# A new unit order, shared row slots and single softmax passes in a grouped-query attention forward and backward kernel

## The chip, the cores and the metric

The kernel runs on one core of a Trainium2 chip. The metric is device time in microseconds (us). Repeated runs of one kernel agree within about 0.3%. "Before" is the kernel before the change, "after" the kernel with it. The granted TensorE clock was 0.98 of full speed.

A few names for the reader. The core has a matrix engine (PE, with PEld for its weight loads), a vector engine (DVE), a scalar engine (ACT), a small general one (POOL), and SP, which here only issues DMA transfers, in program order, to one queue. A queue hands each transfer to 16 DMA engines. "Landing" is the moment when one of those 16 reports its share of a transfer as done.

## The reference, cut to what matters

```python
B, Hq, Hkv, Sq, Sk, D = 32, 32, 4, 4, 2048, 128          # all bf16

def _fwd_reference(q, k, v):
    k = jnp.repeat(k, Hq // Hkv, axis=1)
    v = jnp.repeat(v, Hq // Hkv, axis=1)
    scores = jnp.einsum("bhqd,bhkd->bhqk", q, k) * D ** -0.5
    p = _softmax(scores, axis=-1)
    return jnp.einsum("bhqk,bhkd->bhqd", p, v)

def reference(q, k, v, grad_out):
    out, vjp = jax.vjp(_fwd_reference, q, k, v)
    return (out, *vjp(grad_out))                          # out, dq, dk, dv
```

K and V are 2 MiB each per batch (four heads of 2048 x 128), and so are dK and dV. The rest is small. So 136.31 MB must be read and 136.31 MB written, and a batch moves a little over 8 MiB.

## The kernel before

The work of a batch is cut into units: LK and LV load K and V, each in two rows of 1 MiB (128 partitions x 8 KB); KT and VT transpose them on PE; S makes the scores, MX their maximum, EX the exponential, L the sum and its reciprocal; O and DQ are the small outputs; DV and DK make dV and dK in PSUM; units that end in "e" copy PSUM to SBUF on ACT or DVE; DVs and DKs store. The order of all units, over all batches and engines, is fixed by tables of times.

```python
CAP = dict(q=4, k=8, v=4, qdt=4, kt=8, vt=7, e=2, ..., out=6)     # buffers of each kind
PERIOD = 21.3
PLACE = dict(LK=[-16.977, -14.467], LV=[3.599, 0.95], ..., DVs=[39.32, 39.758], DKs=[48.837, 48.854], ...)
SHIFT = { 0: ..., 1: ..., 2: ..., -4: ..., -3: ..., -2: ..., -1: ... }   # corrections, first and last batches
... # SWAP, BANK: engine and PSUM bank of each unit

def plan(n_batches):
    ...
            u.at = b * PERIOD + PLACE[name][i] + (SHIFT[special][name][i] if special in SHIFT else 0.0)
    ...
    return sorted(order, key=lambda u: u.at), bank_of

        if name in ("LK", "LV"):
            ...
            for w in (slice(0, C * D), slice(C * D, row)) if b == 0 else [slice(0, row)]:
                nc.sync.dma_start(out=x[:, w], in_=src[g][b][:, w])
        ...
        elif name == "MX":                       # twice a batch, two PSUM banks (1024 columns) each
            nc.vector.tensor_scalar(out=spent, in0=t["S", i][:], scalar1=-scale,
                                    scalar2=t["m"][:] if i else None, op0=ALU.mult, op1=ALU.min, accum_out=m[:])
        elif name == "EX":                       # twice a batch
            nc.scalar.activation(out=t["e"][:, 2 * QW * i:2 * QW * i + 2 * QW], in_=t["S", i][:], func=ACT.Exp,
                                 bias=t["m"][:], scale=scale, accum_out=t["l2"][:, i:i + 1])
        elif name == "L":
            nc.vector.reduce_sum(out=lsum[:], in_=t["l2"][:], axis=AX.X)
            ...
        elif name in ("O", "DQ"):                # many small matmuls
            for c in range(4 * i, 4 * i + 4):
                for h in range(NH):
                    nc.tensor.matmul(t[name][r, 0:D], lhsT=left[:, j % 4, r, odd], rhs=right[:, j, :, odd], ...)
        ...
        elif name in ("DVh", "DKh"):             # the last batch only: stores in halves
            nc.sync.dma_start(out=heads_of(out)[:, :, c], in_=heads_of(x)[:, :, c])
        elif name in ("DVs", "DKs"):
            nc.sync.dma_start(out=(dv_r if name == "DVs" else dk_r)[g][b][:, 0:row],
                              in_=staged(b, name[:2])[g][:, 0:row])
```

All loads and stores go through `nc.sync`, one queue in program order. A store that waits for its data therefore also holds up every load behind it. K has 8 rows of buffer, V 4, and dV and dK together 6. Both kernels give PE 8768 matmuls, each preceded by a weight load: 17,536 instructions.

## Time and profile before

| | before |
|---|---|
| time, median of 4 runs | 680.97 us (680.24 to 681.62) |
| profiled span | 678.7 us |
| busy PE, ACT, DVE | 596.6, 593.0, 556.1 us |
| bytes by the data queue | 272.65 MB, 97.6% of 16 engines' span |

The page of the profiled run, before. Part 1 is busy time with its share of the span, part 2 the span in 40 equal slices of 17 us (GB/s is what the DMA engines moved in each), part 3 the queues (q1 carries the data, q8 is the queue that fetches PE's instructions), part 5 the groups of instructions:

```profile
span 678.7 us, 20970 instructions
PE 596.6 (88%) x8768; PEld 409.5 (60%) x8768; DVE 556.1 (82%) x777; ACT 593.0 (87%) x921; POOL 39.5 (6%) x102
...
GB/s 348 398 388 388 424 424 421 426 422 425 423 424 425 424 425 423 424 424 424 426 423 426 423 425 423 418 410 421 424 424 417 421 376 396 352 360 317 400 268 316
...
q1 hardware_dynamic: 39472, 272.65, 97.6%
q8 instruction: 68, 1.11, 0.6%
...
L409 ACT ACTIVATE e_sb<-psum,m 128x1024 bf16<-128x1024 f32 x64 | 71.1, 1121 | 6.5 <-DVE kt_sb L400 6.2
L400 DVE TENSOR_SCALAR_CACHE_REDUCE kt_sb<-psum,m 128x1024 bf16<-128x1024 f32 x32 | 41.1, 1283 | 9.4 <-PE psum L393 5.0
```

No compute engine is busy more than 88% of the span, and the data queue is at 97.6%: this kernel is limited by its transfers. The strip says where it is worse than that. Slices 4 to 31 move 421 to 426 GB/s with few exceptions; the first four move 348 to 398, and the last eight 268 to 400. The Trainium skill ("DMA: Bandwidth & Descriptors", section Bandwidth) gives 425 GB/s for a 16 MB transfer of a single core, so the middle looks as if nothing could be had there.

The last 84 us more closely, in the DMA view of that stretch (each of the 40 slices is 2.1 us):

```profile
DMA  9999999999409999999999998798104999989960
GB/s 377 428 267 413 294 384 415 423 430 418 188 23 374 381 302 409 365 300 413 431 430 417 417 433 376 298 423 341 52 20 195 433 393 369 378 326 389 380 220 2
```

And what SP's queue waited for from 530 us to the end (in total, how often, the longest):

```profile
SPq L499 <- DVE dk_sb L487: 31.6, 4, 13.9
SPq L499 <- ACT dk_sb L487: 22.5, 5, 8.6
SPq L499 <- ACT dv_sb L487: 22.5, 6, 7.8
```

L499 is the store of dV and dK. In the tail the stores wait up to 13.9 us for their data, loads stand behind them, and near 618 and 655 us the DMA engines move almost nothing (23, then 52 and 20 GB/s).

### The profile page before, as it was taken

Reading aid. Unit: us, or ns where it says so; the run is one execution under the profiler, and the core shown is the slowest. Engines: PE = TensorE matmul, PEld = TensorE weight load, DVE = VectorE, ACT = ScalarE, POOL = GpSimd, SP = SyncE. Lnnn points to the kernel's source line nnn. Section 1 sums busy time; section 2 is a strip of 40 time slices with the busy share of each in tenths; the row PEclk is TensorE's granted clock in tenths of the full one; section 3 lists DMA queues with packets and bytes.
Section 4 is the critical chain, followed back from the end, with each engine's and each line's share of the span. In section 5 each row is a group of like instructions: output and inputs, shape, how many; then the busy total and the mean of one; then the engine's idle time right before and its main releaser. Section 6 shows DMA issues by size and latency. Waiting matters only on the chain. (4 is left out here: it accounts for less than half of the span.)

```text
span 678.7 us, 20970 instructions
## 1 busy us (share of the span) xinstructions
PE 596.6 (88%) x8768; PEld 409.5 (60%) x8768; DVE 556.1 (82%) x777; ACT 593.0 (87%) x921; POOL 39.5 (6%) x102
## 2 busy tenths in 40 slices
PE   4989999999999898988899888899888887987995
PEld 3656666666666665656566656666556654655653
DVE  2799899888888888788888888788888884886896
ACT  2799999999999888988889988899988895986994
POOL 0000000000000000000000000000000000000000
PEclk9899999999999999999999999899999996997999
DMA  9999999999999999999999999999999999998968
GB/s 348 398 388 388 424 424 421 426 422 425 423 424 425 424 425 423 424 424 424 426 423 426 423 425 423 418 410 421 424 424 417 421 376 396 352 360 317 400 268 316
DMA packets 39568, 273.98 MB, mean 404 GB/s; under 512 B 4657, under 2 KB 4657, under 8 KB 7729
## 3 DMA queue, kind: packets, MB, share of 16 engines
q1 hardware_dynamic: 39472, 272.65, 97.6%
q8 instruction: 68, 1.11, 0.6%
q14 instruction: 28, 0.22, 0.1%
HBM read 136.31 MB, written 136.31 MB: 402 GB/s over the span
## 5 line engine op out<-in xcount | busy, mean ns | idle before, releaser
L382 PE MATMUL psum<-ident,v_sb 128*128 128x128 f32 x1024 | 153.5, 283 | 24.6 <-DMA v_sb<-in_v_dram 22.4
L487 ACT CAST dk_sb<-psum 128x1024 bf16<-128x1024 f32 x159 | 159.6, 1035 | 16.9 <-PE psum L482 15.2
L487 ACT CAST dv_sb<-psum 128x1024 bf16<-128x1024 f32 x155 | 152.3, 1035 | 2.7 <-PE psum L482 2.5
L382 PEld LDWEIGHTS psum<-ident,v_sb 128*128 128x128 f32 x1024 | 114.2, 143 | 66.9 <-issue 32.8
L382 PE MATMUL psum<-ident,k_sb 128*128 128x128 f32 x1024 | 145.0, 281 | 9.1 <-ACT dk_sb L487 8.0
L382 PEld LDWEIGHTS psum<-ident,k_sb 128*128 128x128 f32 x1024 | 114.2, 142 | 34.8 <-ACT dk_sb L487 19.9
L487 DVE CAST dv_sb<-psum 128x1024 bf16<-128x1024 f32 x101 | 122.6, 1218 | 2.8 <-PE psum L482 1.8
L487 DVE CAST dk_sb<-psum 128x1024 bf16<-128x1024 f32 x97 | 115.7, 1219 | 2.5 <-PE psum L482 2.2
L341 ACT COPY kt_sb<-psum 128x512 f32<-128x512 f32 x190 | 107.8, 601 | 6.5 <-PE psum L382 6.0
L472 DVE SCALAR_TENSOR_TENSOR ds_sb<-psum,delta,e_sb 128x1024 bf16<-128x1024 f32 x64 | 82.1, 1282 | 26.5 <-ACT vt_sb L341 21.3
L341 ACT COPY vt_sb<-psum 128x512 f32<-128x512 f32 x131 | 76.2, 604 | 26.5 <-PE psum L382 24.9
L344 DVE COPY vt_sb<-psum 128x1024 bf16<-128x1024 bf16 x125 | 82.9, 681 | 1.7 <-PE psum L382 1.1
L409 ACT ACTIVATE e_sb<-psum,m 128x1024 bf16<-128x1024 f32 x64 | 71.1, 1121 | 6.5 <-DVE kt_sb L400 6.2
L482 PE MATMUL psum<-e_sb,dop_sb 32*128 32x512 bf16 x512 | 62.5, 385 | 8.9 <-ACT dv_sb L487 8.3
L482 PE MATMUL psum<-ds_sb,qp_sb 32*128 32x512 bf16 x512 | 63.8, 387 | 2.9 <-DVE ds_sb L472 1.5
L344 DVE COPY kt_sb<-psum 128x1024 bf16<-128x1024 bf16 x66 | 44.9, 686 | 16.4 <-PE psum L382 16.1
L417 POOL TENSOR_SCALAR dop_sb<-k_sb,rinv 128x128 bf16<-128x128 bf16 x32 | 20.0, 626 | 613.5 <-PE psum L432 437.6
L400 DVE TENSOR_SCALAR_CACHE_REDUCE kt_sb<-psum,m 128x1024 bf16<-128x1024 f32 x32 | 41.1, 1283 | 9.4 <-PE psum L393 5.0
L432 PE MATMUL psum<-ident,ds_sb 128*128 128x128 f32 x256 | 41.2, 286 | 7.8 <-ACT e_sb L409 7.6
L482 PEld LDWEIGHTS <-dop_sb 32*128 32x128 bf16 x512 | 19.1, 91 | 43.1 <-issue 39.6
L446 PE MATMUL psum<-k_sb,dt_sb 128*32 128x128 bf16 x2048 | 43.5, 221 | 1.8 <-DVE dk_sb L487 0.7
L446 PEld LDWEIGHTS <-dt_sb 128*32 128x32 bf16 x2048 | 37.7, 95 | 11.3 <-issue 8.2
(42 smaller groups left out, 525.3 us busy)
## 6 DMA issues: line engine op xcount, KB each, us to landing
v_sb<-in_v_dram SPq DMA_DIRECT2D x62, 1024.0 KB, 20.4
k_sb<-in_k_dram SPq DMA_DIRECT2D x31, 1088.0 KB, 20.4
out_dram<-dk_sb SPq DMA_DIRECT2D x32, 1024.0 KB, 19.4
out_dram<-dv_sb SPq DMA_DIRECT2D x31, 1056.0 KB, 18.5
k_sb<-in_k_dram SPq DMA_DIRECT2D x31, 1024.0 KB, 20.4
out_dram<-dv_sb SPq DMA_DIRECT2D x31, 1024.0 KB, 20.4
out_dram<-dk_sb SPq DMA_DIRECT2D x30, 1056.0 KB, 18.1
v_sb<-in_v_dram SPq DMA_DIRECT2D x4, 512.0 KB, 8.5
```

The source lines that it names most:

```text
L341: nc.scalar.copy(out=out.rearrange("p c d -> p (c d)").bitcast(FP32), in_=in_.rearrange("p c d -> p (c d)").bitcast(FP32))
L344: nc.vector.tensor_copy(out=out, in_=in_)
L382: nc.tensor.transpose(out=ps[:, j, :], in_=src[:, 4 * i + j, :], identity=ident32[:])
L400: nc.vector.tensor_scalar(out=spent, in0=t["S", i][:], scalar1=-scale, scalar2=t["m"][:] if i else None, op0=ALU.mult, op1=ALU.min, accum_ ...
L409: nc.scalar.activation(out=t["e"][:, 2 * QW * i:2 * QW * i + 2 * QW], in_=t["S", i][:], func=ACT.Exp, bias=t["m"][:], scale=scale, accum_o ...
L417: nc.gpsimd.tensor_scalar(out=t["dop"][:], in0=t["go"], scalar1=t["rinv"][:], scalar2=None, op0=ALU.mult)
L432: nc.tensor.transpose(out=ps[:, j, :], in_=src[:, 4 * i + j, :], identity=ident32[:])
L446: nc.tensor.matmul(t[name][r, 0:D], lhsT=left[:, j % 4, r, odd], rhs=right[:, j, :, odd], start=(c == 0), stop=(c == C - 1), tile_position ...
L472: nc.vector.scalar_tensor_tensor(out=t["ds"][:, w], in0=t["DP", i][:], scalar=t["dl"][:], in1=t["e"][:, w], op0=ALU.subtract, op1=ALU.mult)
L482: nc.tensor.matmul(accs[h // 2][:, QW * (h % 2):QW * (h % 2) + QW], lhsT=t[rhs][r, :], rhs=t[lhs][r, QW * i:QW * i + QW], start=True, stop ...
L487: copy(out=heads_of(staged(b, name[:2])[g])[:, :, QW * i:QW * i + QW], in_=t[name[:2], i][g][:].rearrange("p (h c) -> p h c", h=2))
```

## The change

The change replaces the tables by one string with the order of all 3232 units. Loads and stores now alternate (per batch: SV0, LK1, SK0, LV1, LK0, SK1, SV1, LV0). K, V, dV and dK share 20 row slots in place of separate pools. MX and EX each take one pass over four PSUM banks, so the extra sum goes. q rides on one K row and grad_out on the other, out on a dV row and dq on a dK row, so the last batch's halves and the extra dq transfer go: 260 transfers in place of 267. The number of bytes and of matmuls is the same.

```diff
-CAP = dict(q=4, k=8, v=4, ..., out=6)
-PERIOD = 21.3
-PLACE = dict(...)
-SHIFT = {...}
-SWAP = {...}
-BANK = [...]
+SLOTS, E_TILES, DS_TILES = 20, 2, 2
+TILES = dict(KT=8, VT=7, ET=2, DT=2)
+PLAN = (
+    "a000a110b120a030b040a150e400f4A0e011f0A0e702f7A0e513f5A0b160a070e224f2A0e135f1D0c000d0D0e316f3A0g720h7A0e637f6A0"
...
+slots = [const_pool.tile([P, LONG], BF16, name=f"row{i}") for i in range(SLOTS)]
...
         elif name == "MX":
-            nc.vector.tensor_scalar(out=spent, in0=t["S", i][:], scalar1=-scale,
-                                    scalar2=t["m"][:] if i else None, op0=ALU.mult, op1=ALU.min,
-                                    accum_out=m[:])
+            nc.vector.tensor_scalar(out=t["e"][:], in0=t["S"], scalar1=-scale, scalar2=None, op0=ALU.mult,
+                                    op1=ALU.min, accum_out=t["m"][:])
         elif name == "EX":
-            nc.scalar.activation(out=t["e"][:, 2 * QW * i:2 * QW * i + 2 * QW], in_=t["S", i][:], func=ACT.Exp,
-                                 bias=t["m"][:], scale=scale, accum_out=t["l2"][:, i:i + 1])
-        elif name == "L":
-            nc.vector.reduce_sum(out=lsum[:], in_=t["l2"][:], axis=AX.X)
+            nc.scalar.activation(out=t["e"][:], in_=t["S"], func=ACT.Exp, bias=t["m"][:], scale=scale,
+                                 accum_out=t["l"][:])
...
-        elif name in ("DVh", "DKh"):
-            ...
-        elif name in ("DVs", "DKs"):
-            ...
+        elif name in ("SV", "SK"):
+            n = LONG if i else ROW
+            nc.sync.dma_start(out=(dv_r if name == "SV" else dk_r)[i][b], in_=t["D" + name[1], "out", i][:, 0:n])
```

## The prediction

> **What bounds the kernel now.** The DMA queue. The page shows the queue at 97.6% of 16 engines' span, 272.65 MB in a 678.7 us span, and the 40-slice strip shows 421 to 426 GB/s in most slices from 5 to 31. The Trainium skill ("DMA: Bandwidth & Descriptors", section Bandwidth) gives 425 GB/s for large single-core transfers; this trace agrees (424), so the body is at the queue's rate. In the list of DMA issues, the middle batches (200 to 540 us) repeat every 20.52 us, each transfer of 1 MiB landing about 2.45 us (loads) or 2.6 us (stores) after the one before, seven others always outstanding (latency 20.4 us = 8 transfers). Compute is faster: from 110 to 205 us, when it set the pace, a batch took 19.3 us. Busy per batch: PE 18.6, ACT 18.5, DVE 17.4 us.
>
> **Where time is lost now.** 32 x 20.52 = 657 us is the estimated pure queue time; the span is 678.7. The loss is at both ends: 398, 388, 388 GB/s in slices 1 to 4, and 376, 396, 352, 360, 317, 400, 268, 316 in the last eight. In the tail the SP queue waits for stores' data (single waits of 8 to 14 us) while loads stand behind it in order; the backlog falls to nothing near 572, 582, 594, 619, 648 and 658 us, and PE twice waits 4 to 6 us for k_sb.
>
> **What the change does.**
> - Bytes: unchanged (272.6 MB). The middle cannot get faster than the queue.
> - Loads and stores alternate mostly one by one, and 20 rows are shared by K, V, dV and dK in place of 8+4+6 in separate pools. Loads stay roughly 2.5 batches ahead. This should keep the queue filled in the head and most of the tail: the main gain.
> - One EX over 2048 columns: two cost 2 x (1121+209) ns; one about 2200 (estimate from the column slope of the ACT copies, 0.85 ns; "ScalarE: Activation LUTs" gives 280 + 0.833 N ns, and 1121 at N=1024 agrees). Saves about 0.45 us of ACT a batch. One MX saves about 0.3 us of DVE, the removed sum 0.15. All of it is off the critical path while the queue is the limit; 7 of 16 wide copies now go to DVE (before 6.2), which gives DVE's saving back.
> - Price: S holds four of eight banks for about 5 us of a batch. I expect the order to hide it.
>
> **Sum.** 1.8 us to the first byte + 657 + about 3 us after the last store's issue + 1.9 us between span and time = 663 us; gain about 17 us, nearly all at the two ends. Remaining losses: slow packets as seen now in head and tail (up to 8 us).
>
> **What would show it.** Batch period in the middle still 20.2 to 20.6 us; DMA strip 420 or more from slice 1 or 2 to about slice 36; no wait of PE for k_sb over 3 us; ACT busy below 580 us, DVE about 555 to 575; EX near 2.0 us + 0.2, MX near 2.3 us.
>
> **What would make it wrong.** The four-bank S stage or static order lifts the compute period above 20.5 us (then 675 or more); the alternating loads and stores run at another rate than runs of two or three (either way); in-order stores still block loads in the last four batches; slow packets persist.
>
> Predicted 663 us, 655 to 673; faster by over 2% 0.68, within 2% 0.30, slower 0.02.

## The result, and the profile after

| | before | after |
|---|---|---|
| time, median of 4 runs | 680.97 us (680.24 to 681.62) | 672.70 us (672.46 to 672.85) |
| profiled span | 678.7 us | 671.1 us |
| last landing of the last transfer | 677.6 us | 670.0 us |
| busy PE, ACT, DVE | 596.6, 593.0, 556.1 us | 607.9, 569.6, 572.0 us |

The ratio is 0.9879, with a 95% interval of 0.9861 to 0.9896. Ratios here are the mean time of one kernel's fast runs over that of the other's of the same rounds, so they are not quite the ratio of the medians quoted. In later rounds the same kernel came to 671.76 us (671.42 to 672.66, 4 runs), against 680.76 for before: 0.9869 (0.9850 to 0.9887). Executions over 1.5% slower than the fastest of the same kernel are left out of the means. So the gain is 1.2 to 1.3%, about 8 to 9 us. I had expected 17.

The same lines of the page, after:

```profile
span 671.1 us, 20678 instructions
PE 607.9 (91%) x8768; PEld 401.4 (60%) x8768; DVE 572.0 (85%) x736; ACT 569.6 (85%) x802; POOL 39.0 (6%) x102
...
GB/s 354 417 424 423 419 381 423 423 423 423 423 426 424 424 423 424 424 425 426 414 420 425 413 417 421 414 422 424 396 388 408 417 424 424 404 421 423 347 258 322
...
q1 hardware_dynamic: 37440, 272.65, 98.2%
q8 instruction: 69, 1.13, 0.6%
...
L241 PE MATMUL psum<-ident,row 128*128 128x128 f32 x2048 | 290.1, 284 | 28.4 <-DMA row<-in_k_dram 21.5
...
L260 DVE TENSOR_SCALAR_CACHE_REDUCE e_sb<-psum 128x2048 bf16<-128x2048 f32 x32 | 73.3, 2292 | 5.7 <-PE psum L255 5.7
...
L264 ACT ACTIVATE e_sb<-psum,m 128x2048 bf16<-128x2048 f32 x32 | 64.0, 2001 | 0.2 <-DVE e_sb L260 0.2
```

The head is better: slices 1 to 3 went from 398, 388, 388 to 417, 424, 423. In the tail only the last three slices are clearly low. But new dips have come: 381 in slice 5, and 396, 388, 408 in slices 28 to 30. The exponential took 2001 ns in place of two times 1121 (before: 64 passes, now 32). The skill ("ScalarE: Activation LUTs", section "What ACT_TABLE_LOAD costs") states about 280 ns + 0.833 ns per column, or about 1990 at 2048 columns; this trace agrees.

The last 76 us after the change, in the DMA view (slices of 1.9 us):

```profile
DMA  9999999999999999995884899921085599999930
GB/s 423 428 393 419 424 435 425 420 427 420 420 424 423 428 433 422 421 405 237 371 328 169 355 422 420 414 104 35 31 345 224 213 400 418 422 410 397 430 156 4
```

SP's queue, 530 us to the end:

```profile
SPq L320 <- DMA out_dram<-row: 26.7, 13, 2.2
SPq L226 <- DMA out_dram<-row: 20.9, 5, 4.9
SPq L320 <- DVE row L316: 18.8, 3, 7.8
SPq L320 <- DVE row L296: 10.0, 3, 5.1
```

L320 is a store, L226 a load. What SP waits for longest in the tail is now earlier stores (26.7 and 20.9 us), that is the queue itself. The waits of stores for their data, all lines of the view added up, fell from about 95 to 42 us, the longest from 13.9 to 7.8. As far as SP's waits go, the order does what it was made for. Where, then, is the other half of the expected gain?

### The profile page after: what moved, and what is told of

Its sections match the earlier page's. It is cut to its first block, busy times and chain, and to the rows that moved or that the text cites. A ratio compares the mean times of both kernels' runs of the same rounds, so it can differ in the third digit from the quotient of the medians.

```text
span 671.1 us, 20678 instructions
## 1 busy us (share of the span) xinstructions
PE 607.9 (91%) x8768; PEld 401.4 (60%) x8768; DVE 572.0 (85%) x736; ACT 569.6 (85%) x802; POOL 39.0 (6%) x102
## 4 chain that ended last, share of the span: by engine, by line
DMA 50%; PE 37%; DVE 4%; ACT 4%; issue 3%; SPq 0%; POOL 0%; DVEq 0%; ACTq 0%; POOLq 0%
DMA row<-in_k_dram 50%; PE psum L241 19%; PE psum L310 8%; PE psum L288 5%; PE psum L255 5%; ACT row L316 3%; DVE vt_sb L209 2%; DVE ds_sb L303 1%; DVE row L316 0%; DVE e_sb L260 0%; ACT e_sb L264 0%; PE psum L230 0%; SPq L226 0%; ACT dt_sb L207 0%; DVE row L296 0%
## 5 line engine op out<-in xcount | busy, mean ns | idle before, releaser
L241 PE MATMUL psum<-ident,row 128*128 128x128 f32 x2048 | 290.1, 284 | 28.4 <-DMA row<-in_k_dram 21.5
L316 ACT CAST row<-psum 128x1024 bf16<-128x1024 f32 x292 | 289.2, 1023 | 30.9 <-PE psum L310 29.1
L241 PEld LDWEIGHTS psum<-ident,row 128*128 128x128 f32 x2048 | 224.7, 143 | 94.8 <-issue 32.0
L316 DVE CAST row<-psum 128x1024 bf16<-128x1024 f32 x220 | 264.9, 1217 | 5.7 <-PE psum L310 2.9
L207 ACT COPY kt_sb<-psum 128x512 f32<-128x512 f32 x190 | 110.2, 598 | 20.6 <-PE psum L241 20.4
L260 DVE TENSOR_SCALAR_CACHE_REDUCE e_sb<-psum 128x2048 bf16<-128x2048 f32 x32 | 73.3, 2292 | 5.7 <-PE psum L255 5.7
L264 ACT ACTIVATE e_sb<-psum,m 128x2048 bf16<-128x2048 f32 x32 | 64.0, 2001 | 0.2 <-DVE e_sb L260 0.2
L288 PE MATMUL psum<-row,dt_sb 128*32 128x128 bf16 x2048 | 43.5, 222 | 6.2 <-issue 5.6
L255 PE MATMUL psum<-vt_sb,qdt_sb 128*32 128x512 bf16 x512 | 40.7, 388 | 4.6 <-issue 4.5
L207 ACT COPY dt_sb<-psum 128x512 f32<-128x512 f32 x63 | 38.4, 611 | 1.0 <-PE psum L241 0.9
L288 PEld LDWEIGHTS <-et_sb 128*32 128x32 bf16 x2048 | 30.4, 95 | 13.8 <-ACT et_sb L207 11.3
```

The source lines that it names most:

```text
L207: nc.scalar.copy(out=out.bitcast(FP32), in_=in_)
L241: nc.tensor.transpose(out=ps[:, P * j:P * j + P], in_=src[:, 4 * half + j, :], identity=ident32[:])
L255: nc.tensor.matmul(out[r, QW * w:QW * w + QW], lhsT=t["qdt"][:, P * side + 32 * h:P * side + 32 * h + 32], rhs=t[x, NH * i + h][:, QW * w: ...
L260: nc.vector.tensor_scalar(out=t["e"][:], in0=t["S"], scalar1=-scale, scalar2=None, op0=ALU.mult, op1=ALU.min, accum_out=t["m"][:])
L264: nc.scalar.activation(out=t["e"][:], in_=t["S"], func=ACT.Exp, bias=t["m"][:], scale=scale, accum_out=t["l"][:])
L288: nc.tensor.matmul(t[name][r, :], lhsT=left[:, j, r, odd], rhs=right[:, 4 * i + j, :, odd], start=(i == 0 and c == 0), stop=(i == 1 and c ...
```

## The experiments

### What there was to explain

Each transfer counts 16 landings, one per DMA engine. The Trainium skill ("DMA: Bandwidth & Descriptors", section "Why a DMA increments its semaphore by 16 and not by 1") explains the 16: one increment from each engine that carries a share. I had used only the last of the 16, since that is what the consumer waits for. Listing all 16 shows something that no strip shows. This is the distance in us from the first landing of a transfer to the sixteenth, read from the semaphore updates in the trace (transfers are counted in the order of issue):

```
transfer             0    30    60    90   120   150   180   210   240   last
before             0.7   2.9   5.3   8.2  11.2  13.5  13.4  14.6   9.3    1.2
after              0.6   2.2   5.1   9.0  12.3  12.6  13.2  12.9  12.7    1.8
after, 15th only   0.5   1.8   3.1   4.3   5.6   5.3   5.4   6.5   5.7    1.7
```

In both kernels one engine of the 16 falls steadily behind the rest, until it is 12 to 14 us late. The spread stops growing there, and the trace shows why. The transfers use eight semaphores in turn, and in both kernels every transfer is issued only after the one eight places before it has landed on all 16 (252 of 252 in after, 259 of 259 in before). So at most eight are outstanding, and once the late engine is that far behind, the others run out of work and wait for it: transfer 150 of after has its first landing 5.2 us after its issue and its sixteenth 17.8 us after. At the end the late one works alone: in the trace of after the data packets come one at a time from 645.4 to 650.6 us and from 653.3 to 655.0 us. The first of these is the hole of 31 to 104 GB/s in the strip above, which I would have put down to a starved queue; the second makes the slices of 224 and 213. In before one engine is alone from 618.4 to 620.5 and from 655.5 to 657.8 us, in the two holes shown of its tail; the data queue stands still only from there to 659.2 us.

So there were two explanations. **Lagging engine**: something takes time on one DMA engine, and the kernel lasts as long as that engine's own work; holes elsewhere only show the others waiting for it. A likely something is the fetching of instructions: the page lists them as a queue of their own (q8: 69 packets of 16 KB). **Order**: the loss is stores waiting for data and loads behind them, as the prediction has it, and what is left needs a still better order. Smaller rivals: the four-bank passes cost as much as they saved; or another transfer order has another rate.

The expectations below use their own words for the theories of that time.

### Transfers alone, in the order of after (e1)

Only loads and stores are issued, with the same order, slots and sizes. Twenty small fills at the start keep the stored memory initialised.

```diff
         for u in units:
-            emit(u)
+            if u.name in ("LK", "LV", "SV", "SK"):
+                emit(u)
```

> The same 260 transfers in the same order and slots, no compute (results wrong on purpose). Seen in both traces: of the 16 landings of one transfer the last comes 12 to 14 us after the first by the middle of the run, so one of the 16 DMA engines lags. Theory A (that engine has extra work, the instruction fetches of PE, and its own total is the kernel's time): 640 to 652 us, first and last landing of a transfer under 2 us apart all along. Theory B (that engine is slower by itself): 664 to 672 us, 10 us or more apart. Theory C (the rest of the time is the order's waits for compute): 640 to 652 us, and the landings still 10 us or more apart.

Measured: 647.29 us (647.13 to 647.45, 2 runs). Its output is wrong, which doesn't matter for the time. The page:

```profile
span 645.7 us, 365 instructions
...
GB/s 340 424 427 419 425 423 427 428 427 425 429 428 427 428 427 426 428 427 427 428 427 427 427 427 428 425 428 428 428 427 428 427 429 427 428 426 429 427 427 331
...
q1 hardware_dynamic: 37440, 272.65, 100.3%
```

No engine lags: from first to sixteenth landing it is 3.4 us at most, all run long. And the queue needs 647 us, not the 657 of the prediction. The strip looks almost like the middle of the two kernels, 427 or 428 in place of 424; the difference that matters is not in it, because it is an average over 16 engines. The landings show it. Between transfer 30 and transfer 210 the last landing advances by this much per eight transfers:

```
                           us per 8 transfers (one batch)
transfers alone (e1)       (522.4 -  72.7) / 22.5 = 19.99
before                     (541.6 -  77.5) / 22.5 = 20.63
after                      (542.3 -  73.2) / 22.5 = 20.85
```

Both kernels lose 0.6 to 0.9 us in every batch of the middle, which I had taken for the queue's own rate.

### Transfers alone, in the order of before (e3)

The same with the transfers of the kernel before: its order, its 8 + 4 + 6 row buffers, its halves at the end.

```diff
         for u in order:
-            if u.on or not u.eng:
+            if (u.on or not u.eng) and u.key[1] in ("LK", "LV", "DVs", "DKs", "DVh", "DKh", "DQs"):
                 emit(u)
```

> The kernel before with its transfers alone: its order, its sizes (halves at the end included), its 8 + 4 + 6 row buffers, no compute; wrong on purpose. It asks whether part of the 8.2 us that the change won is a better rate of alternating loads and stores, a risk that the prediction named, or whether the order of the transfers has nothing to do with the queue's rate. Theory A (kernel time is the queue's even time plus instruction fetch on one engine plus what is lost at the ends while the queue waits for data): the same as the changed kernel's transfers alone, 646 to 650 us, about 427 GB/s in the middle, all 16 landings of a transfer within 3 to 4 us. Rival (runs of two or three loads or stores cost more than alternation): 652 us or more; or, if runs are cheaper, under 644 us.

Measured: 649.02 us (648.42 to 650.07, 4 runs). It is 1.7 us above e1. Its output is wrong, which doesn't matter for the time. The spread between a transfer's landings stays at 5.0 us or less.

```profile
span 648.3 us, 328 instructions
...
GB/s 341 424 425 415 424 412 426 427 428 427 425 428 425 427 428 427 429 427 429 427 428 428 428 427 427 428 427 427 427 427 427 428 427 428 428 428 427 428 425 283
```

So alternating loads and stores is no faster for the queue than runs of two or three, a risk that the prediction had named. The 1.7 us (2.7 us between the last landings of the two profiled runs, where e3's was the slowest of its four) are the most that the transfers themselves, with fewer small ones at the end, can have contributed.

With these two runs each kernel can be held against its own transfers alone. The table gives, at equal bytes, how many us later the last landing came than in the transfers-alone run (e3 for before, e1 for after), with the number of PE instruction blocks (16 KB, 256 instructions) fetched by then in after:

```
MiB moved   27.4   57.9   118.8   149.3   210.2   230.6   240.7   250.8   260
before       5.0    5.9    10.9    12.9    17.0    21.8    24.3    26.0   30.3
after        0.5    5.4    12.5    14.5    19.8    21.1    21.8    23.7   25.4
PE blocks      6     15      32      39      56      61      64      66     69
```

After 27 MiB the change is 4.5 us ahead. By 58 MiB it has only 0.5 left, and by 210 MiB it is 2.8 us behind. From there to the end before loses 13.3 us and after 5.6. The gain of the change is the tail, and what the head gains is given back in the middle.

One store explains part of the giving back. The queue view of after from 60 to 105 us, and the DMA view from 80 to 105 us (slices of 0.6 us):

```profile
SPq L320 <- ACT row L316: 19.2, 6, 10.0
```

```profile
GB/s 422 425 426 431 391 243 412 395 419 406 302 315 380 419 419 429 350 270 230 203 284 379 433 433 433 433 419 433 431 424 421 420 419 433 419 419 422 428 390 444
```

One store waits 10.0 us for its eviction. When it is issued at 83.0 us only 0.44 MiB are left to move, and the engines run thin until 94 us. Between transfers 30 and 60 the first landings lose 2.5 us on e1. This is the dip of slice 5, and it is a real loss by order.

### Transfers with PE instructions beside them (e2)

e1 plus two matmuls of 128 columns for each unit, on constants, waiting for no data: 6464 matmuls, or 12,928 PE instructions with their weight loads.

```diff
+            for j in range(2):
+                nc.tensor.matmul(psum[:, 0:P], lhsT=ident[:], rhs=ident[:], start=True, stop=True)
```

> The same queue with 6464 small matmuls beside it that wait for nothing and that nothing waits for: as many PE instructions as the real kernel (12928). Theory A: 15 to 25 us more than without them (660 to 672 us), and the landings of a transfer 8 us or more apart while PE runs. Theories B and C: the time of the queue alone, within 3 us.

Measured: 661.48 us (661.41 to 661.54, 2 runs): 14.2 us more than e1 in the same rounds. Its output is wrong, which doesn't matter for the time.

```profile
span 659.8 us, 13293 instructions
PE 362.6 (55%) x6464; PEld 362.4 (55%) x6464; DVE 10.3 (2%) x21; POOL 0.7 (0%) x6
...
PE   9999999999999999999999000000000000000000
...
q8 instruction: 50, 0.82, 0.5%
```

PE touches none of the transferred data here. One engine still falls behind: 3.4 us of spread at transfer 30, 6.9 at 60, 13.0 at 120. PE ends at 364 us, and from then on nothing more is lost; the last landing is 14.1 us behind e1 at transfer 150, and 14.1 at the end. The lag itself is not made up either, as one expects of an engine that has as much to do as the others and began the rest of it late.

### As much PE work in a quarter of the instructions (e7)

Is it PE's work that disturbs the queue, its reading of SBUF, say, or the number of its instructions? One matmul of 512 columns on every second unit has about the same busy time with a quarter of the instructions.

```diff
+            if n % 2:
+                nc.tensor.matmul(psum[:, 0:4 * P], lhsT=ident[:], rhs=wide[:], start=True, stop=True)
```

> The queue alone with 1616 matmuls of 512 columns (3232 PE instructions, a quarter of those of the run with PE beside the queue, about the same PE columns). Theory A (instruction fetch makes the lag): 3 to 5 us over the queue alone, 650 to 652 us. Rival (PE reading SBUF slows the DMA engine): 658 to 663 us.

Measured: 650.76 us (650.46 to 651.07, 2 runs). That is 3.5 us above e1, a quarter of e2's 14.2. Its output is wrong, which doesn't matter for the time. (e7 ran in another round, on another chip than e1 and e2; the last landings in the two traces, 648.2 and 644.6 us, give 3.6 us.)

```profile
PE 348.8 (54%) x1584; PEld 158.5 (24%) x1616; DVE 10.8 (2%) x22; POOL 0.7 (0%) x6
...
q8 instruction: 12, 0.20, 0.1%
```

PE was busy as long (349 against 363 us; some of its 1616 matmuls are missing in the record). The cost followed the number of instructions: 14.2 us for 12,928 in e2, 3.5 us for 3232 here, 1.1 ns each. So beside the bare queue it is this number that makes the lag, and not PE's busy time.

Is it then their fetching, as I took it to be? The skill says, in "Runtime: NRT & Kernel Launch", section "Instruction fetch mechanics", that a sequencer drives its own DMA queue, refilled in blocks of 16 KiB, and that crossing a block is "mostly hidden". The trace agrees on the blocks, and PE, idle for 1.4 us in all of e2, loses nothing by them. They do reach the data: in e2 each of the 50 fetches is followed, within 20 ns of its end, by a data packet of 0.67 to 0.87 us (the usual is 0.31). But the engines that this sets back are others than the late one. These are all 16 landings of transfer 120, in us after the first:

```
e1    0.0  0.2  0.2  0.2  0.2  0.3  0.4  0.8  1.3  1.4  1.6  1.8  1.9  2.0  2.1  2.2
e2    0.0  0.1  0.1  0.2  0.2  0.3  0.6  6.2  6.2  6.3  6.4  6.4  6.4  6.6  8.1 13.0
```

Eight engines are some 6 to 8 us late in e2. In the transfers before and after, they fall back one after another, by some 1.2 to 1.7 us, one at each fetch. Their lateness does not reach that of the sixteenth, and so costs no time. The sixteenth loses in another way. This is by how much its landing came later after the landing before it than in e1 (e1's median for a transfer of the same kind and size; for before, e3's), on the mean, with single steps of over 0.3 us counted apart:

```
run, transfers               us per store   us per load   steps: number, us in all
e1, 10 to 258                    0.00           0.00          4,  1.8
e2, 30 to 139 (PE busy)          0.21           0.00          2,  1.1
e2, 141 to 258 (PE done)         0.00           0.01          1,  0.7
e7, 30 to 139 (PE busy)          0.04           0.01          2,  1.0
e8, 30 to 258 (next section)    -0.02          -0.01         47, 30.9
before, 40 to 209                0.13           0.00          8,  4.3
after, 40 to 209                 0.14           0.01         12,  6.7
e9, 40 to 209                    0.14           0.01          4,  2.5
```

In e2 it loses about 0.2 us at every store, nothing at loads, and has no step of a fetch's size at any PE block of that stretch (its two steps are 0.7 us, with a packet of q14, and 0.4); when PE is done, the loss stops. In before and after the same loss at stores is the largest part. So the fetches of PE's blocks are not what makes this engine late. What ties the number of PE instructions to the stores of one engine stays open. A rival that no run excludes is the profiler: every run was profiled, and its trace lists every instruction, so its work grows with their number too.

### ACT's instructions in place of PE's (e8)

```diff
+            for j in range(2):
+                nc.scalar.copy(out=junk[0:1, j:j + 1], in_=ident[0:1, j:j + 1])
```

> The queue alone with 6464 one-element ACT copies (half the instructions of the PE stream). If ACT's instructions are fetched through the same DMA engine as PE's, about half of the 14.2 us that the PE stream added: 652 to 656 us. If each instruction stream has another engine: lag of one engine as well, the same 652 to 656. If only PE's fetch costs the queue: 646 to 649 us.

Measured: 730.10 us (730.10 to 730.11, 2 runs), and a miss: the kernel became limited by ACT itself, which I had not worked out beforehand. Its output is wrong, which doesn't matter for the time.

```profile
DVE 10.3 (1%) x21; ACT 726.8 (100%) x6465; POOL 0.7 (0%) x6
...
q14 instruction: 53, 0.43, 0.1%
```

The time says nothing then, but the queue's own end does: its last landing came at 674.2 us, 29.6 us after e1's, and one engine lagged 14 us again. The blocks are smaller here (8 KB), and there are 49 of them by the last landing (two of these e1 has as well), so one cost about 0.6 us. Here the fetches are the cause, as the table above shows: the late engine loses nothing at ordinary stores, but has 47 steps, 30.9 us in all, and 41 of them (26.7 us) come with the fetch of a block. So these blocks do fall on the late engine. In the real kernel q14 fetched 24 such packets, from several engines' streams; of the 17 between transfers 40 and 209 of after only three come with a step (2.0 us).

### After with fewer PE instructions (e9)

The same test within the real kernel: O and DQ do two of their eight steps, with wrong out and dq. That removes 6144 PE instructions, and 24 to 25 blocks.

```diff
-            for c in range(8):
+            for c in (0, 7):
```

> The kernel after with 4 of 16 chunks of the O and DQ products (out and dq wrong on purpose): 3072 matmuls and their weight loads less, 6144 PE instructions, 24 blocks of 16 KB. The runs beside the queue alone gave 14.2 us for 50.5 blocks and 3.5 us for 12.6, so 0.28 us a block. Theory A (one DMA engine's work, with the fetches, is the limit): 6 to 7 us less than after, 665 to 668 us. Rival (the order of compute, above all PE at 91% busy, limits): PE loses about 10% of its busy time, 650 us or less. Rival (neither): 672.

Measured: 667.03 us (666.00 to 667.48, 4 runs), against 671.76 for after in the same rounds.

```profile
PE 589.6 (89%) x5696; PEld 370.1 (56%) x5696; DVE 571.0 (86%) x736; ACT 570.3 (86%) x802; POOL 39.0 (6%) x102
...
q8 instruction: 44, 0.72, 0.4%
```

The time lies within the range expected of theory A, but the trace shows that most of the gain is of another kind. The DMA view of e9 from 80 to 105 us, where after had its stall:

```profile
GB/s 419 434 410 399 416 431 443 426 435 433 419 433 433 421 423 426 416 432 433 419 405 419 406 433 433 431 430 427 424 420 433 419 446 421 423 426 415 431 430 440
```

The stall is gone, though one store still waits 10.0 us for its data. Against after in the same rounds (e12), e9's last landing is 1.2 us behind at transfer 30, 2.3 us ahead at 60, 3.4 at 240 and 4.7 at the end. So 3.5 us were won where the stall had been, 1.3 us at the end, and only 1.1 us in the 180 transfers between, where e2's 1.1 ns per instruction would give about 4.7 (an estimate). The late engine's loss at stores, 0.14 us, is that of after. PE's work did shrink too (about 18 us of its busy time), which can act on the order. That the number of PE instructions sets the lag of the real kernel is therefore not shown by this run; that the range was met is luck.

### Is it the order of the passes? After with two passes again (e4)

```diff
-            nc.vector.tensor_scalar(out=t["e"][:], in0=t["S"], ...)
+            for j, to in enumerate((m0, t["m"])):       # two passes of 1024 columns, MX and EX
+                w = slice(2 * QW * j, 2 * QW * j + 2 * QW)
+                nc.vector.tensor_scalar(out=t["e"][:, w], in0=t["S"][:, w], ...)
...
+            nc.vector.reduce_sum(out=t["l"][:], in_=t["l2"][:], axis=mybir.AxisListType.X)
```

> Undoes one part: the max and the exp run in two passes of two banks each again, with the sum of the two parts; order and slots as after. ACT gets about 0.45 us and DVE about 0.5 us more a batch. Theories A and B (the queue is the limit): within 0.3% of after, 671 to 675 us. Rival (the compute chain through the four-bank stage is the limit): 0.9 us a batch or more, 695 us or more.

Measured: 672.53 us (671.88 to 673.22, 4 runs), correct; ratio to before 0.9874 (0.9847 to 0.9901), against 0.9879 for after. ACT has 64 exponentials of 1147 ns in place of 32 of 2001, and nothing follows. The single passes are worth nothing in time that these runs could see, and cost nothing; they lie off the critical path, as predicted.

### Which engine lags? (e5, e6)

The skill states, in "DMA: Bandwidth & Descriptors", section "Latency and other measured facts", that engines 7 and 15 are usually slower in traces. The page's section on the 16 says which engines a transfer takes: the largest number up to 16 that divides its rows, the lowest-numbered first. So a store of 120 + 8 rows leaves engine 15 with nothing to do. I cut eight of the stores like that.

```diff
+            for r in (slice(0, 120), slice(120, P)) if (name, i) == ("SV", 0) and b % 4 == 2 else (slice(0, P),):
+                nc.sync.dma_start(out=to[r], in_=x[r, 0:n])
```

> Eight of the 260 transfers (the first dV row store of every fourth batch) are issued as 120 rows and 8 rows, which by the Trainium skill puts them on the 15 and the 8 lowest-numbered engines: engine 15 gets 64 rows less (64 x 0.305 us = 19.5 us), engines 0 to 7 get 8 rows more (2.4 us). If one lagging engine is the limit and it is number 15: 655 to 664 us. If it is one of 0 to 7: 674 to 676. If it is one of 8 to 14: 672 to 673. Theory C: 672 to 673 whichever it is.

Measured: 678.12 us (676.61 to 682.38, 4 runs), correct. That is about 5.5 us slower than after, and no theory had foreseen it. Then a probe: after with sixteen tiny loads, of 1, 2, ... 16 rows, in the middle of the run, where the spread had reached 12 us.

```diff
+            if on and k < 16 and u.name in ("LK", "LV", "SK", "SV"):
+                k += 1
+                nc.sync.dma_start(out=probe[0:k, at:at + k + 2], in_=k0[0][0:k, 0:k + 2])
```

> The kernel after, with 16 very small loads between the transfers of the middle, of 1 row, 2 rows, ... 16 rows (6 to 36 bytes a row, every size once). By the Trainium skill a transfer of k rows uses the k lowest-numbered engines, so the first k whose last small packet starts 10 us or more after its first names the lagging engine as number k-1. Run e5 had no gain from sparing engine 15. Theory A1 (one fixed engine of 0 to 7 lags): a jump at one k of 2 to 8, and for every larger k. A2: a jump at 9 to 15. If no k shows a jump, the lag moves between engines.

Measured: 672.92 us (1 run, of unknown state), correct. The start of the last tiny packet of each load after its first one, in us:

```
rows     1     2     3     4     5     6     7     8     9    10    11    12    13    14    15    16
us       0   1.9   1.5   0.4   6.4   5.5   5.6   5.6   5.4   5.6   5.7   5.7   5.8   5.5   5.6   6.2
```

Up to four rows the last starts within 1.9 us, with four within 0.4 us; from five rows on, one is 5.4 us late or more. If k rows use the k lowest-numbered engines, as the skill has it, the late one is the fifth, number 4. The step at five agrees with that numbering, and it is not engine 7 or 15. The probe also did something by accident. The sixteen tiny loads take places among those outstanding, and the spread fell from 12 to 5.8 us while they passed, and grew to 13.6 us again by transfer 260. The time did not change (672.92 us). How far the fifteen run ahead is of no account, then; the late engine's own work sets the time.

### Relieving the late engine, and a control (e10, e11)

Sixteen stores cut into 112 + 4 + 4 + 4 + 4 rows (e10): the pieces of four rows go to the lowest four engines, so engine 4 should be spared part of them. As a control, the same sixteen stores cut into 112 + 16 rows (e11), which divides evenly over all sixteen.

```diff
+            cuts = (0, 112, 116, 120, 124, P) if (name, i, b % 2) == ("SV", 0, 1) else (0, P)    # e10
+            cuts = (0, 112, P) if (name, i, b % 2) == ("SV", 0, 1) else (0, P)                   # e11
+            for r in map(slice, cuts[:-1], cuts[1:]):
+                nc.sync.dma_start(out=to[r], in_=x[r, 0:n])
```

> The probe run pointed to the fifth lowest engine as the one that lags. Sixteen dV row stores (row 0 of every second batch) are cut into 112 rows and four times 4 rows, so that the four lowest engines get 11 rows and all others 7 in place of 8. The fifth gets 16 rows less, 16 x 0.305 = 4.9 us; the four lowest 48 rows more, 14.6 us, of about 19 us that they have to spare. Theory A with engine 4: 667 to 669.5 us. If the laggard is another, or moves: 672 or more.

> The control for the run before: the same sixteen stores cut into 112 and 16 rows, by which every engine keeps its 8 rows. Every theory: 672 to 674 us; more than that is what a cut itself costs.

Measured, both correct: of e10's six runs two (701.4 and 701.5 us) were slow; the four fast ones ran from 674.56 to 681.36, median 675.67, ratio to before 0.9939 (0.9906 to 0.9972). e11 took 678.57 us (676.29 to 679.73, 6 fast runs), ratio 0.9960 (0.9940 to 0.9980). Both expectations missed. The control shows that cutting a store costs time in itself: 678.57 - 671.76 = 6.8 us for 16 cuts, about 0.4 us each (why, no run shows; each piece takes one of the eight places for outstanding transfers). At that rate e5's eight cuts account for some 3.4 of its 5.5 us (an estimate), and the cost of cutting swallows whatever e10 relieved: the two intervals overlap. So that engine 4 can be relieved at a profit is neither shown nor refuted.

### After once more, beside e9 to e11 (e12)

The kernel of after unchanged, so that the three above have it in the same rounds.

> The kernel after unchanged, in the same rounds, as the base for the three others: 672 to 673 us.

Measured: 671.76 us (671.42 to 672.66, 4 runs), 0.9869 of before. The spreads of its landings are those of the first run (1.9 us at transfer 30, 12.6 at 120, 13.1 at 210). No experiment gave a correct kernel that beats it.

## Why the prediction was right or wrong

It was wrong in size: it said 663 us, a gain of 17 (2.6%), and 8 to 9 us (1.2 to 1.3%) came. 672.7 us lies within the range given, at its edge.

**The step that failed** is "the body is at the queue's rate", with its number, "32 x 20.52 = 657 us is the estimated pure queue time". The pure queue time, measured by itself, is 647.3 us for the changed kernel's transfers and 649.0 for those of before. In the middle the queue alone advances a batch in 19.99 us, before in 20.63 and after in 20.85. The plateau was not the queue's rate but the pace of one late DMA engine. Most of the difference is what this engine loses at stores: 0.14 us at each in after, which for 128 stores gives 18 us, an estimate. Of the 25.4 us that after lies behind its transfers alone, this is the larger part. A further 2.5 us is the stall at 83 to 94 us. The rest, some 5 us, is not assigned: the late engine's single steps and what the last stores wait for are candidates. Why the engine loses at stores is open. Beside the bare queue PE's instructions bring the loss about, in proportion to their number (e2, e7); in the real kernel a third fewer of them left it as it was (e9).

**Why it failed.** I took a plateau in a kernel that runs at 424 GB/s, found a page of the skill that says 425, and called it the limit. The same queue without compute moves 427 to 428. Under one per cent in a mean of sixteen engines hid one engine that was losing 0.1 us or so with every transfer. Having put 657 us in the sum for the queue, I was left with 678.7 - 657 = 22 us "at both ends" and believed that 17 of them could be had. With before's own 0.13 us at 128 rows stored, some 17 us (an estimate), its transfers need 649 + 17 = 666 us. If that loss stays whatever the order, an order could save about 15 us, and the change saved 8 of them.

**"The loss is at both ends"** holds for before's loss by order: 5.0 us in the first 27 MiB and 13.3 us from 210 MiB on, with the late engine's loss in both. The tail was the part that paid: 13.3 became 5.6. The head's 4.5 us were won, and given back by 210 MiB: 2.5 us of that in the new stall at 83 us, the rest in a lag that simply had not come up yet when the queue was idle for other reasons. My reading is that a lagging engine catches up while the others are idle; take the idle time away and the lag appears.

**"The middle cannot get faster than the queue"** was true as a sentence and misapplied. The middle got slower, 20.63 to 20.85 us a batch, and it was not at the queue's own rate in either kernel.

**"Batch period in the middle still 20.2 to 20.6 us"**: missed, 20.85 from transfer 30 to 210.

**"DMA strip 420 or more from slice 1 or 2 to about slice 36"**: right at the head (417, 424, 423) and wrong at slice 5 (381) and 28 to 30 (396, 388, 408). The first is the stall after the store that waits 10.0 us. That the later dips come from the fifteen engines waiting for the late one fits the spread of 12.9 us there, but no run shows it alone.

**"No wait of PE for k_sb over 3 us"**: PE waited 21.5 us for K rows in all, in 15 waits, the longest 4.4 us. Missed by a little.

**The single passes "off the critical path"**: right. e4 takes them away and the time stays (672.53 us). The sizes were right too: the exponential 2001 ns ("near 2.0 us"), MX 2292 ns ("near 2.3"), ACT busy 569.6 us ("below 580"), DVE 572.0 ("555 to 575").

**"The alternating loads and stores run at another rate"**, named as a risk: refuted by e3 against e1, 649.0 and 647.3 us, with the small pieces at the end inside the difference.

**"In-order stores still block loads in the last four batches"**, named as a risk: partly so. The longest such wait fell from 13.9 to 7.8 us; the tail still has holes, but for some 6.9 us of them one engine is at work alone and the hole is not a loss by order.

**"Slow packets persist"**, named as a risk: partly so. What data packets took above 309 ns per 8 KB summed to 16.0 us per engine in before, 13.8 in after, 7.0 in e2 and 2.8 in e1. In e2 two kinds can be told apart: the 50 long packets that follow the fetches, and some 500 packets more than in e1 that are 9 to 60 ns too long, which add up to 14.5 us and stop when PE does. The second kind fits the loss of the late engine at stores. For before and after nobody has sorted them.

## What to carry to other kernels

Before calling a queue's plateau its limit, run the kernel's transfers alone in their own order: here one edit gives 649 us for before's 681, and shows that the middle loses time too. Look at all sixteen landings of a transfer, not only the last: a mean rate 1% under the best can hide one engine that is 13 us late and sets the time. Then ask at which transfers the late engine loses: here a cause that fitted in size, the fetching of PE's instructions, did not fit in place. Beside a full queue, many small matmuls cost time by their number (14.2 against 3.5 us, e2 and e7); in the kernel itself a third fewer of them brought 1.1 us in the middle (e9). Small cuts of large stores are not free.

## What the Trainium skill lacked or had wrong

- "Runtime: NRT & Kernel Launch", section "Instruction fetch mechanics", calls the cost of crossing a 16 KiB block "mostly hidden". For PE it was (idle 1.4 us in e2). For the DMA engines it was not: each of e2's 50 blocks was followed by a data packet of 0.67 to 0.87 us in place of 0.31 and set one of eight engines back, in turn, by some 1.2 to 1.7 us.
- The same section gives blocks of 16 KiB for every engine. ACT's instructions came in packets of 8 KB (e8), and 41 of them came with a step of the one late engine, 26.7 us in all, about 0.65 us each.
- No page that I read says that a stream of PE instructions can make one DMA engine slower at stores: 0.21 us per store of 1 MiB in e2, 0.04 in e7 with a quarter of the instructions, 0.00 at loads in e2. Why is open, the profiler included.
- "DMA: Bandwidth & Descriptors", section "Latency and other measured facts", names engines 7 and 15 as usually slower; it calls its reason a guess and ties it to DMAs issued by way of GpSimd, which this kernel doesn't use. In this kernel's traces the probe's step lies at five rows (1.9 us at most up to four, 5.4 us or more from five on), which points to engine 4, 12 to 14 us late in the full kernel.
- The same page, section Bandwidth, gives 425 GB/s at 16 MB, measured there with loads issued from GpSimd. Here 260 transfers of about 1 MiB, loads and stores in turn, moved 427 to 428 GB/s for most of the middle of e1. Small as it is, the difference misled the prediction.
- The same page's rules for kernel authors advise one 128-partition transfer in place of two halves, but no page that I read says what cutting a 128-row store costs when the queue is full: 16 such cuts cost 6.8 us (e11), about 0.4 us each.
